# Key tiles of later batches: half tiles sent together with the queries, or quarter tiles sent one by one between them

## The chip, the cores and the metric

The kernel runs on one core of a Trainium2 chip. The metric is the device time of one execution in microseconds (us). A profiled execution was also taken; its trace gives the rows below. TensorE is called PE, VectorE DVE, ScalarE ACT, GpSimd POOL, SyncE SP. ACT and SP also issue DMAs; where a row says ACTq or SPq it is that issuing, not work of the engine.

## The reference

Four batches. In each, 12288 queries of 128 channels attend to 768 keys, which are 4x4 means of a 384x32 map times a weight; keys and values are the same. Of each batch's output rows the 128 with the highest gate score go through a small MLP and are replaced.

```python
kv_pool = kv.reshape(B, H // r, r, W // r, r, C).mean(axis=(2, 4))   # r = 4
k = v = kv_pool.reshape(B, -1, C) @ w_sr
a = softmax(q @ k.transpose(0, 2, 1) / sqrt(C)); x = a @ v
scores = einsum('bsd,d->bs', x, w_gate)                              # per batch: top 128 rows
out[top] = x[top] + sigmoid(scores[top]) * (relu(x[top] @ w1) @ w2)
```

## The kernel before

A batch is 48 blocks of 256 queries, so there are 192 blocks, numbered i = 0 to 191 through all batches. In block i PE makes the scores of block i+1 (tile `s`) and multiplies the weights of block i-4 with the values (`AV`, tile `o_two`). In between, DVE takes the row maxima (`m`), ACT the exponentials (`am`) and their high 16-bit half, and POOL the low half (both in `hl`). PE needs them transposed (`at`): 10 of the 12 128x128 tiles of each half go through a transposing DMA from SP (`turn`, two per block: the high half, then the low one), in the last batch all 12. A block's `at` must have landed when its AV begins, four blocks after its scores were used. There are five `at` buffers. SP also sends the finished rows (`out`, 256 KB, in every odd block).

Work of the next batch runs beside the blocks of the present one. Its keys come in KT = 6 tiles of 1 MB (`kv_raw`, three buffers). POOL adds the 16 taps of each key (`kv_sum`, six steps, one per block, of which the first three read `kv_raw`), so a tile takes six blocks: in batch 0 tile kc of batch 1 is read at the ends of blocks 6kc, 6kc+1 and 6kc+2; in later batches this starts five blocks into the batch. PE projects the sum (`key_tile`), and after the last tile POOL splits the values (`vx`).

Queries come 256 KB at a time (`load_q`), issued by ACT at the start of every even block, six blocks ahead. Tiles 0 to 2 of batch 1 are loaded by SP at the beginning. The other 15 tiles (`load_kv` with parts=-2) come as two halves of 512 KB, issued by ACT: the first where the generator `next_keys` reaches the tile before (two tiles before in batch 1), the second where h is 3, two blocks later; for tile 0 of batches 2 and 3 both lie in the first blocks of the batch before. Each half has a semaphore of its own (`own_load`), and POOL waits for it just before its first and second read (`landed`). The order on each engine is the order in which the code is written (`InOrder`); nothing reorders it.

Of the kernel before, what the change touches and what calls it, by code (L numbers as in the profile page):

```python
# [6 lines left out]
F32 = mybir.dt.float32  # L7
# [12 lines left out]
P = 128  # L20
B, N, C = 4, 12288, 128
HK, WK, R = 384, 32, 4
M = (HK // R) * (WK // R)
KT = M // P
TAPS = R * R
# [5 lines left out]
NBLK = N // BLK  # L31
# [40 lines left out]
def attention_topk_mlp(ctx, tc, a, outs, capacity):  # L72
    nc = tc.nc
    pe, dve, act, pool, sp = (InOrder(tc, e) for e in (nc.tensor, nc.vector, nc.scalar, nc.gpsimd, nc.sync))
# [3 lines left out]
    kvp = ctx.enter_context(tc.tile_pool(name="kvp", bufs=3))  # L78
# [49 lines left out]
    loads = {}  # L128

    def own_load(lane, out, in_):  # L130
        if lane not in lanes:
            lanes[lane] = [tc.alloc_semaphore(f"{lane[0]}{lane[1]}"), 0]
        sem = lanes[lane]
        r = act.dma_start(out=out, in_=in_)
        r.then_inc(sem[0], 16)
        sem[1] += 16
        tc.no_tile_sem_insts.add(r.ins.name)
        tc.add_to_no_dep_group(r.ins.name, r.ins)
        return sem[0], sem[1], r.ins.name

    def landed(engine, load):
        sem, count, group = load
        r = engine.wait_ge(sem, count)
        tc.declare_fence(r.ins, group=group)
        return r.ins

    def load_kv(b, kc, parts=1, t=None):
        late = t is not None
        if not late:
            t = kvp.tile([P, 2, P // 2, TAPS], F32, name="kv_raw")  # L150
        n = 2 // abs(parts)
        for i in range(abs(parts)):
            out, in_ = t[:, i * n:(i + 1) * n], a["kv"][:, b, kc, i * n:(i + 1) * n]
            if parts > 0:
                sp.dma_start(out=out, in_=in_)
            elif late == (i > 0):
                loads[b, kc, i] = own_load(("kv", (KT * b + kc) % 3 * 2 + i), out, in_)
        return t

    qraw = {}  # L160

    def load_q(b, ch, lo=0, hi=CHUNK):
        if (b, ch) not in qraw:
            qraw[b, ch] = qp.tile([P, CHUNK], F32, name="q_raw")
        out, in_ = qraw[b, ch][:, lo:hi], a["q"][:, b, ch, lo:hi]
        if (b, ch) == (0, 0):
            sp.dma_start(out=out, in_=in_)
        else:
            assert hi - lo == 2 * BLK
            blk = ch * BPC + lo // BLK  # L170
            loads[b, blk] = own_load(("q", blk // 2 % 3), out, in_)
# [201 lines left out]

    def next_keys(b):
        new_keys(b)
        raws = {}
        ready = None

        def after(kc):
            if kc % 2:  # L380
                pair = kc // 2
                start(vals, values(b, pair))
                start(splits, round_k(b, 2 * pair))

        lead, wait = (2, 0) if b == 1 else (1, 5)
        raws[0] = load_kv(b, 0, 1 if b == 1 else -2)
        if b == 1:
            raws[1] = load_kv(b, 1)
        for k in range(wait):
            yield "d"  # L390
            if k == 2:
                load_kv(b, 0, -2, raws[0])
        for kc in range(KT):
            nxt = kc + lead if kc + lead < KT and (kc or b > 1) else 0
            if nxt:
                raws[nxt] = load_kv(b, nxt, -2)
            t = raws[kc]
            pooled = kvs.tile([P, P], F32, name="pooled")
            u = kvs.tile([P, P, TAPS // 2], F32, name="kv_sum")
            t = t.rearrange("p h k t -> p (h k) t")  # L400
            by8 = [(u[:, lo:hi], t[:, lo:hi, 0:8], t[:, lo:hi, 8:16]) for lo, hi in ((0, 43), (43, 86), (86, P))]
            by4 = [(u[:, lo:hi, 0:4], u[:, lo:hi, 0:4], u[:, lo:hi, 4:8]) for lo, hi in ((0, 86), (86, P))]
            by2 = [(u[:, lo:hi, 0:2], u[:, lo:hi, 0:2], u[:, lo:hi, 2:4]) for lo, hi in ((0, 64), (64, P))]
            adds = [[x] for x in by8] + [[by4[0]], [by4[1], by2[0]], [by2[1], (pooled, u[:, :, 0], u[:, :, 1])]]
            for h, part in enumerate(adds):
                if ready and h == 2:
                    yield from key_tile(b, kc - 1, ready)
                    after(kc - 1)
                yield "d"
                if h < 2 and (b, kc, h) in loads:  # L410
                    landed(pool, loads[b, kc, h])
                for o, x, y in part:
                    pool.tensor_tensor(out=o, in0=x, in1=y, op=ALU.add)
                if kc == 0 and h == 0 and b == 1:
                    raws[2] = ahead.pop()
                if h == 3 and nxt:
                    load_kv(b, nxt, -2, raws[nxt])
            ready = pooled
        for _ in range(2):
            yield "d"  # L420
        yield from key_tile(b, KT - 1, ready)
        after(KT - 1)
# [375 lines left out]

    first_keys()

    select, prep, vals, splits, ended, ahead = [], [], [], [], [], []

    def start(tasks, gen):
        tasks.append([gen, next(gen)])
# [15 lines left out]
    n = nb - 1  # L820
# [43 lines left out]
    for i in range(nb):  # L864
        old = i >= LAG
        b, blk = blocks[i]
        if blk % 2 == 0 and i + AHEAD < nb and i + AHEAD >= BPC:
            nb_, nblk = blocks[i + AHEAD]
            load_q(nb_, nblk // BPC, nblk % BPC * BLK, (nblk % BPC + 2) * BLK)
        if blk == 0 and b + 1 < B:  # L870
            start(prep, next_keys(b + 1))
        if i == 0:
            sp.dma_start(out=w1, in_=a["w1"])
            sp.dma_start(out=w2, in_=a["w2"].rearrange("(t f) d -> f t d", f=P))
            ahead.append(load_kv(1, 2))
        if i:
            borrow(s_flat[(i - 1) % 2])
        s_max(i)
        if old:
            for j in range(QT):  # L880
                AV(i - LAG, j, halves=(0,))
            at_point("pe")
            for j in range(QT):
                AV(i - LAG, j, halves=(1,))
        else:
            at_point("pe")
        if i == 0:
            split_q(*blocks[2])
        InOrder.seen.clear()
        at_point("ev")  # L890
        bank1 = list(InOrder.seen)
        InOrder.seen.clear()
        at_point("up")
        at_point("g")
        more = 0 < i < nb - 1
        bank0 = list(InOrder.seen)
        if more:
            if not old:
                warm(12, s_flat[(i + 1) % 2][:, 1024:1024 + P], bank0 + bank1)
            free = {3: bank0 + bank1, 2: bank0, 1: bank0, 0: ()}  # L900
            for part, term in ((3, LOW), (2, LOW), (3, HIGH), (2, HIGH)):
                S(i + 1, part, term, free[part])
        exp(i, 2 if by_pe(i) else 1)
        if i < nb - 1 and by_pe(i):
            turn_pe(i)
        exp(i, 1 if by_pe(i) else 2)
        if i == nb - 1:
            st[i]["apart"] = turn_last(i, 1024, 2 * M)
            exp(i, 0)
            turn_last(i, M, 1024)  # L910
            turn_last(i, 0, M)
        InOrder.seen.clear()
        at_point("a")
        for x in InOrder.seen:
            for y in st[i + 1]["far"]:
                tc.declare_no_dep(x, y, reason="other banks")
        if more:
            for part, term in ((1, HIGH), (0, HIGH), (1, LOW), (0, LOW)):
                S(i + 1, part, term, free[part])
        to_high(i, 1)  # L920
        if old:
            sums(i - LAG)
            recip(i - LAG)
            at_point("t")
            at_point("k")
            finish(i - LAG)
        else:
            at_point("t")
        at_point("cmp")
        at_point("v")  # L930
        if i == n and quick:
            ranking = floor()
            next(ranking)
        to_low(i, 1, dve)
        if i < nb - 1:
            exp(i, 0)
        to_high(i, 0)
        if i < nb - 1:
            turn(i, 0)
            to_low(i, 0, pool)  # L940
            turn(i, 1)
        else:
            to_low(i, 0, dve)
        if i % 2 and i + 3 < nb:
            split_q(*blocks[i + 3], both=False)
        elif i % 2 == 0:
            advance(splits)
        if i and i + 3 < nb:
            low_q(*blocks[i + 3])
        at_point("d")  # L950
        if old and blocks[i - LAG][1] == NBLK - 1:
            start(select, topk(blocks[i - LAG][0]))
    ended.append(True)
    room["select"], room["count"] = banks[1], banks[0][:, 0:1]
    b = blocks[n][0]
# [237 lines left out]
```

## Time and profile before

| | us |
|---|---|
| median of three executions | 923.22 (922.45 to 926.89) |
| profiled execution | 917.34 |
| its span, first to last instruction | 915.5 |
| PE busy | 862.9 (94%) |
| DVE / ACT / POOL busy | 783.4 / 743.6 / 762.6 |

The profiled execution is the one that all rows describe: it lasted 1.84 us more than its span. PE works nearly without a break, so an idle stretch of PE in the middle is time of the kernel, whereas an idle stretch of another engine need not be.

### The profile page before, as it was taken

The numbers are of one execution on the slowest core, as the hardware profiler recorded it, in microseconds if no ns is written. First come the engines' busy times: TensorE is split into PE (matmuls) and PEld (weight loads), VectorE is DVE, ScalarE is ACT, GpSimd is POOL, SyncE is SP. The second block draws the span as 40 slices with busy tenths as digits, with TensorE's granted clock in tenths as the row PEclk, the third lists the DMA queues.
The fourth block names the chain that finished last, engine by engine and source line by source line (L and its number), as shares of the span: only waits on it lengthen the run. The fifth ranks groups of instructions, "written<-read, shape, count | busy, mean of one in ns | idle before, by whom it ended". The sixth has DMA issues, their size and how long they took to land.

```text
span 915.5 us, 21496 instructions
## 1 busy us (share of the span) xinstructions
PE 862.9 (94%) x7679; PEld 685.6 (75%) x7799; DVE 783.4 (86%) x1936; ACT 743.6 (81%) x1148; POOL 762.6 (83%) x597
## 2 busy tenths in 40 slices
PE   3898899999999999999999999999999998999996
PEld 3576777777777777777777877777777776777776
DVE  6786788888889898999878999999988998999973
ACT  2787778888888888888887888888888998989951
POOL 2698979988979999999878999999889787777752
PEclk9999999999999999999999999999999999999999
DMA  8999999999999999999999999999999999999990
GB/s 316 302 204 214 211 227 235 231 206 205 237 237 242 237 264 221 253 250 221 207 212 222 239 261 234 235 260 231 223 192 229 235 227 243 251 255 242 235 209 28
DMA packets 560479, 210.22 MB, mean 230 GB/s; under 512 B 528720, under 2 KB 530000, under 8 KB 559728
## 3 DMA queue, kind: packets, MB, share of 16 engines
q1 hardware_dynamic: 542480, 168.29, 93.6%
q10 hardware_dynamic: 17568, 39.85, 16.9%
q8 instruction: 62, 1.02, 0.5%
q0 software_dynamic: 320, 0.66, 0.3%
q14 instruction: 49, 0.40, 0.2%
HBM read 52.04 MB, written 25.49 MB: 85 GB/s over the span
## 4 chain that ended last, share of the span: by engine, by line
PE 64%; DVE 9%; DMA 9%; ACT 7%; POOL 5%; issue 4%; SPq 0%; ACTq 0%; DVEq 0%; POOLq 0%; another core or an unknown queue 0%
PE s L57 33%; PE o_two L57 31%; DMA at<-hl 7%; DVE m L57 4%; ACT am L57 4%; POOL hl L57 3%; DMA kv_raw<-in_kv 2%; ACT hl L57 2%; ACT s L57 1%; DVE o_two L57 1%; POOL ql L57 1%; DVE hl L57 1%; POOL kv_sum L57 1%; DVE junk L57 1%; DMA xe<-out,idx 1%
## 5 line engine op out<-in xcount | busy, mean ns | idle before, releaser
L57 POOL TENSOR_TENSOR hl<-am,hl 128x1280 bf16<-128x1280 f32 x191 | 501.7, 2627 | 103.4 <-ACT hl L57 49.8
L57 PE MATMUL o_two<-vx,at 128*128 128x259 f16 (+1 forms) x4548 | 424.3, 246 | 17.7 <-DMA at<-hl 11.2
L57 PEld LDWEIGHTS <-at 128*128 128x128 f16 (+1 forms) x4656 | 364.0, 97 | 98.4 <-DMA at<-hl 15.5
L57 ACT ACTIVATE am<-s,m 128x512 f32<-128x512 f32 (+1 forms) x530 | 358.9, 705 | 41.7 <-DVE m L57 26.4
L57 DVE TENSOR_REDUCE m<-s 128x2 f32<-128x1536 f32 x192 | 336.9, 1755 | 13.3 <-PE s L57 11.0
L57 ACT CAST hl<-am 128x1280 f16<-128x1280 f32 x191 | 240.6, 1260 | 6.1
L57 PE MATMUL s<-kb,ql 128*128 128x512 bf16 (+1 forms) x735 | 229.0, 324 | 4.7 <-issue 0.2
L57 PE MATMUL s<-kh,qh 128*128 128x512 f32 (+1 forms) x769 | 216.3, 377 | 1.4 <-ACT kh L57 0.7
L57 PE MATMUL s<-kl,qh 128*128 128x256 bf16 (+1 forms) x683 | 211.9, 322 | 1.2
L57 POOL TENSOR_TENSOR ql<-q_raw,qh 128x256 bf16<-128x256 f32 (+1 forms) x190 | 140.2, 738 | 2.0 <-ACT qh L57 2.0
L57 DVE TENSOR_REDUCE o_two<-o_two 128x258 f32<-128x516 f32 x188 | 128.4, 683 | 0.0
L57 PEld LDWEIGHTS s<-kh,qh 128*128 128x128 f32 x769 | 116.8, 191 | 7.0 <-ACT kh L57 0.9
L57 PEld LDWEIGHTS <-qh 128*128 128x128 bf16 x769 | 75.0, 98 | 55.3 <-issue 30.1
L57 ACT CAST at<-s 128x256 f16<-128x256 f32 x147 | 55.6, 378 | 72.5 <-PE s L57 70.4
L57 PEld LDWEIGHTS <-ql 128*128 128x128 bf16 x769 | 75.6, 98 | 25.7 <-issue 0.3
L57 DVE TENSOR_SCALAR rz<-o_two,sg 128x2 f32<-128x2 f32 x189 | 41.5, 219 | 61.8 <-PE o_two L57 59.7
L57 DVE TENSOR_TENSOR x<-o_two,rz 128x256 f32<-128x256 f32 x189 | 78.4, 415 | 0.0
L57 DVE TENSOR_TENSOR at<-s,at 128x256 bf16<-128x256 f32 x147 | 63.1, 429 | 10.3 <-ACT at L57 5.5
L57 PE MATMUL s<-cst,am 128*128 128x128 f32 x302 | 57.6, 274 | 2.4 <-ACT am L57 2.2
L57 ACT CAST qh<-q_raw 128x512 fp32r<-128x512 f32 x96 | 59.0, 615 | 0.0
L57 POOL TENSOR_TENSOR kv_sum<-kv_raw 128x344 f32<-128x344 f32 (+1 forms) x54 | 49.1, 910 | 0.0
L57 PEld LDWEIGHTS s<-cst,am 128*128 128x128 f32 x302 | 37.8, 140 | 12.2 <-ACT am L57 5.3
(162 smaller groups left out, 522.2 us busy)
## 6 DMA issues: line engine op xcount, KB each, us to landing
out<-x SPq DMA_DIRECT2D x96, 256.0 KB, 4.2
q_raw<-in_q ACTq DMA_DIRECT2D x92, 256.0 KB, 3.8
kv_raw<-in_kv ACTq DMA_DIRECT2D x30, 512.0 KB, 5.1
at<-hl SPq DMA_TRANSPOSE x382, 4.6
kv_raw<-in_kv SPq DMA_DIRECT2D x5, 1024.0 KB, 8.5
kv_raw<-in_kv SPq DMA_DIRECT2D x7, 512.0 KB, 5.4
w<-in_w SPq DMA_DIRECT2D x2, 512.0 KB, 11.4
q_raw<-in_q SPq DMA_DIRECT2D x2, 256.0 KB, 5.8
```

Source lines behind the costliest of these rows:

```text
L57: r = f(*args, **kwargs)
```

## The change

The 15 tiles that ACT loads now come as four quarters of 256 KB, each with its own semaphore (12 for keys in place of 6). They no longer hang on where `next_keys` stands: a table, `stream`, gives one quarter to every odd block: for batch 1 blocks 5, 7, ... 27 (tiles 3 to 5), for batches 2 and 3 blocks 33, 35, ... 127. ACT issues it at the start of the block. POOL waits for quarters 0 and 1 before its first read of a tile, for quarter 2 before the second and for quarter 3 before the third. Bytes, tiles, buffers and the adds themselves are as before.

```diff
         tc.declare_fence(r.ins, group=group)
         return r.ins
 
-    def load_kv(b, kc, parts=1, t=None):
-        late = t is not None
-        if not late:
-            t = kvp.tile([P, 2, P // 2, TAPS], F32, name="kv_raw")
-        n = 2 // abs(parts)
-        for i in range(abs(parts)):
-            out, in_ = t[:, i * n:(i + 1) * n], a["kv"][:, b, kc, i * n:(i + 1) * n]
-            if parts > 0:
-                sp.dma_start(out=out, in_=in_)
-            elif late == (i > 0):
-                loads[b, kc, i] = own_load(("kv", (KT * b + kc) % 3 * 2 + i), out, in_)
-        return t
+    raws = {}
+
+    def load_kv(b, kc):
+        raws[b, kc] = kvp.tile([P, 2, P // 2, TAPS], F32, name="kv_raw")
+        sp.dma_start(out=raws[b, kc], in_=a["kv"][:, b, kc])
+
+    stream = {}
+    for b in range(1, B):
+        for kc in range(3 if b == 1 else 0, KT):
+            for part in range(4):
+                stream[NBLK * (b - 1) + 8 * kc - (19 if b == 1 else 15) + 2 * part] = b, kc, part
+
+    def load_part(b, kc, part):
+        if part == 0:
+            raws[b, kc] = kvp.tile([P, 2, P // 2, TAPS], F32, name="kv_raw")
+        h, k = part // 2, part % 2 * (P // 4)
+        loads[b, kc, part] = own_load(("kv", (KT * b + kc) % 3 * 4 + part), raws[b, kc][:, h, k:k + P // 4], a["kv"][:, b, kc, h, k:k + P // 4])
 
     qraw = {}
 
@@ -373,7 +378,6 @@
 
     def next_keys(b):
         new_keys(b)
-        raws = {}
         ready = None
 
         def after(kc):
@@ -382,19 +386,13 @@
                 start(vals, values(b, pair))
                 start(splits, round_k(b, 2 * pair))
 
-        lead, wait = (2, 0) if b == 1 else (1, 5)
-        raws[0] = load_kv(b, 0, 1 if b == 1 else -2)
         if b == 1:
-            raws[1] = load_kv(b, 1)
-        for k in range(wait):
+            load_kv(b, 0)
+            load_kv(b, 1)
+        for k in range(0 if b == 1 else 5):
             yield "d"
-            if k == 2:
-                load_kv(b, 0, -2, raws[0])
         for kc in range(KT):
-            nxt = kc + lead if kc + lead < KT and (kc or b > 1) else 0
-            if nxt:
-                raws[nxt] = load_kv(b, nxt, -2)
-            t = raws[kc]
+            t = raws[b, kc]
             pooled = kvs.tile([P, P], F32, name="pooled")
             u = kvs.tile([P, P, TAPS // 2], F32, name="kv_sum")
             t = t.rearrange("p h k t -> p (h k) t")
@@ -407,14 +405,10 @@
                     yield from key_tile(b, kc - 1, ready)
                     after(kc - 1)
                 yield "d"
-                if h < 2 and (b, kc, h) in loads:
-                    landed(pool, loads[b, kc, h])
+                for x in ((0, 1), (2,), (3,))[h] if h < 3 and (b, kc, 0) in loads else ():
+                    landed(pool, loads[b, kc, x])
                 for o, x, y in part:
                     pool.tensor_tensor(out=o, in0=x, in1=y, op=ALU.add)
-                if kc == 0 and h == 0 and b == 1:
-                    raws[2] = ahead.pop()
-                if h == 3 and nxt:
-                    load_kv(b, nxt, -2, raws[nxt])
             ready = pooled
         for _ in range(2):
             yield "d"
@@ -798,7 +792,7 @@
 
     first_keys()
 
-    select, prep, vals, splits, ended, ahead = [], [], [], [], [], []
+    select, prep, vals, splits, ended = [], [], [], [], []
 
     def start(tasks, gen):
         tasks.append([gen, next(gen)])
@@ -867,12 +861,14 @@
         if blk % 2 == 0 and i + AHEAD < nb and i + AHEAD >= BPC:
             nb_, nblk = blocks[i + AHEAD]
             load_q(nb_, nblk // BPC, nblk % BPC * BLK, (nblk % BPC + 2) * BLK)
+        if i in stream:
+            load_part(*stream[i])
         if blk == 0 and b + 1 < B:
             start(prep, next_keys(b + 1))
         if i == 0:
             sp.dma_start(out=w1, in_=a["w1"])
             sp.dma_start(out=w2, in_=a["w2"].rearrange("(t f) d -> f t d", f=P))
-            ahead.append(load_kv(1, 2))
+            load_kv(1, 2)
         if i:
             borrow(s_flat[(i - 1) % 2])
         s_max(i)
```

On ACT, in blocks 4 to 6 of batch 0 (`am` is the exponential, `hl` the high half, `qh` a query split), the order before has these rows:

```order
L57 CAST hl<-am 128x1280 [waits DMAHW6_49,DMAHW5_49,Activation_49]
L57 ACTIVATE am<-s_110,m 128x512 [waits DVE_49,Pool_49]
L57 ACTIVATE am<-s_110,m 128x256
L57 CAST at<-s_110 128x256 [waits PE_49]
L57 ACTIVATE am<-s_110,m 128x768
L57 CAST hl<-am 128x1280 [waits DMAHW7_49,DMAHW0_49,Activation_49]
L57 CAST qh<-q_raw 128x512 [waits q1,Activation_sequencer_49]
L57 DMA kv_raw<-in_kv 128x1024 [waits DMAHW2_49,Pool_49]
L57 DMA q_raw<-in_q 128x512
```

and the changed kernel these:

```order
L57 CAST hl<-am 128x1280 [waits DMAHW6_49,DMAHW5_49,Activation_49]
L57 DMA kv_raw<-in_kv 128x512 [waits DMAHW2_49,DMAHW0_49,Pool_49]
L57 ACTIVATE am<-s_110,m 128x512 [waits DVE_49]
L57 ACTIVATE am<-s_110,m 128x256
L57 CAST at<-s_110 128x256 [waits PE_49]
L57 ACTIVATE am<-s_110,m 128x768
L57 CAST hl<-am 128x1280 [waits DMAHW7_49,DMAHW0_49,Activation_49]
L57 CAST qh<-q_raw 128x512 [waits q1,Activation_sequencer_49]
L57 DMA q_raw<-in_q 128x512
```

The key load of 1024 elements per partition that stood right before the query load is gone from there; one of 512 elements stands a block earlier, behind the cast of the even block and before the first exponential of the odd one. ACT has 30 rows more in all.

On POOL, at tile 3 of batch 1 (`kv0`, `kv1`, ... are the key loads' own semaphores), the order before has these rows:

```order
L57 TENSOR_TENSOR kv_sum<-kv_raw 128x344 [waits kv0,Pool_sequencer_49]
L57 TENSOR_TENSOR hl<-am,hl 128x1280 [waits DMAHW2_49,DMAHW1_49,Activation_49]
L57 TENSOR_TENSOR ql<-q_raw,qh 128x256 [waits Activation_sequencer_49,PE_49,Activation_49]
L57 TENSOR_TENSOR kv_sum<-kv_raw 128x344 [waits kv1,Pool_sequencer_49]
L57 TENSOR_TENSOR hl<-am,hl 128x1280 [waits DMAHW4_49,DMAHW3_49,Activation_49]
L57 TENSOR_TENSOR ql<-q_raw,qh 128x256
L57 TENSOR_TENSOR kv_sum<-kv_raw 128x336
```

and the changed kernel these:

```order
L57 TENSOR_TENSOR kv_sum<-kv_raw 128x344 [waits kv0,kv1,Pool_sequencer_49]
L57 TENSOR_TENSOR hl<-am,hl 128x1280 [waits DMAHW2_49,DMAHW1_49,Activation_49]
L57 TENSOR_TENSOR ql<-q_raw,qh 128x256 [waits Activation_sequencer_49,PE_49,Activation_49]
L57 TENSOR_TENSOR kv_sum<-kv_raw 128x344 [waits kv2,Pool_sequencer_49]
L57 TENSOR_TENSOR hl<-am,hl 128x1280 [waits DMAHW4_49,DMAHW3_49,Activation_49]
L57 TENSOR_TENSOR ql<-q_raw,qh 128x256
L57 TENSOR_TENSOR kv_sum<-kv_raw 128x336 [waits kv3,Pool_sequencer_49]
```

No instruction of POOL moves; the waits are four per tile where they were two. The rows of PE, DVE and SP stand in the same order as before.

## Rows read from the trace of the kernel before

**Rows 1.** The page's part 1: engine, busy us, share of the span, instructions.

```profile
PE 862.9 (94%) x7679; PEld 685.6 (75%) x7799; DVE 783.4 (86%) x1936; ACT 743.6 (81%) x1148; POOL 762.6 (83%) x597
```

**Rows 2.** What PE waited for, 45 to 880 us: total us, times, longest.

```profile
PE o_two L57 <- DMA at<-hl: 11.2, 12, 2.6
PE o_two L57 <- POOL vx L57: 3.0, 2, 1.9
```

**Rows 3.** The same for 60 to 120, 280 to 400, and 700 to 880 us.

```profile
PE o_two L57 <- DMA at<-hl: 7.0, 5, 2.6
...
PE o_two L57 <- DMA at<-hl: 1.9, 5, 0.8
...
PE o_two L57 <- DMA at<-hl: 2.2, 2, 1.4
```

**Rows 4.** Timeline of PE at its two longest waits: start, us, operation, [idle before <-releaser].

```profile
87.70 0.85 PE L57 MATMUL o_two<-vx,at 128*128 128x130 f16 x12 [2.63 <-DMA at<-hl]
...
110.68 3.83 PE L57 MATMUL o_two<-vx,at 128*128 128x259 f16 x24 [2.60 <-DMA at<-hl]
```

**Rows 5.** Three stretches: busy us by engine, PE clock, DMA share, GB/s.

```profile
60.30:121.40 61.10, 53.80 (x458) 42.02 (x464) 44.97 (x87) 45.07 (x69) 50.86 (x42) 0.97 1.17 216
130.40:182.50 52.10, 51.68 (x459) 41.41 (x465) 45.04 (x88) 45.05 (x69) 50.48 (x42) 1.00 1.16 232
110.70:114.10 3.40, 3.40 (x20) 2.62 (x21) 0.00 (x0) 0.56 (x2) 3.35 (x3) 0.50 1.20 344
```

**Rows 6.** Row maxima (one per block) in the first two stretches: count, ns, starts.

```profile
L57 DVE TENSOR_REDUCE m<-s x12: 1757/1758/1759, 60.3 to 116.8; 128x2 f32<-128x1536 f32 x12
...
L57 DVE TENSOR_REDUCE m<-s x12: 1758/1758/1759, 130.4 to 178.2; 128x2 f32<-128x1536 f32 x12
```

**Rows 7.** Transposes, 60 to 120 us: issue ns min/median/max, then landing us.

```profile
L57 SPq DMA_TRANSPOSE at<-hl x24: 1282/1834/5197, 56.6 to 119.4; - x24
...
DMA to landing us min/median/max: 3.1/5.5/10.9
```

**Rows 8.** The same, 150 to 240 us, a stretch without key loads.

```profile
L57 SPq DMA_TRANSPOSE at<-hl x43: 1252/1636/3497, 149.1 to 239.9; - x43
...
DMA to landing us min/median/max: 3.1/4.4/6.8
```

**Rows 9.** The same, 280 to 400 us, with nine key loads.

```profile
L57 SPq DMA_TRANSPOSE at<-hl x53: 1271/1647/4193, 279.7 to 398.6; - x53
...
DMA to landing us min/median/max: 3.2/4.9/9.2
```

**Rows 10.** Loads issued by ACT, timeline around 78 us.

```profile
78.08 0.33 ACTq L57 DMA_DIRECT2D kv_raw<-in_kv  x1
78.44 1.32 ACTq L57 DMA_DIRECT2D q_raw<-in_q  x1
```

**Rows 11.** Key loads by ACT, whole kernel; 60 to 120; 280 to 400 us: count, issue ns, starts.

```profile
L57 ACTq DMA_DIRECT2D kv_raw<-in_kv x30: 334/334/825, 52.1 to 609.1; - x30
...
L57 ACTq DMA_DIRECT2D kv_raw<-in_kv x4: 334/334/352, 69.5 to 108.6; - x4
...
L57 ACTq DMA_DIRECT2D kv_raw<-in_kv x9: 334/334/370, 282.3 to 391.0; - x9
```

**Rows 12.** The page's part 6: DMA issues, KB each, median us to landing.

```profile
q_raw<-in_q ACTq DMA_DIRECT2D x92, 256.0 KB, 3.8
kv_raw<-in_kv ACTq DMA_DIRECT2D x30, 512.0 KB, 5.1
```

**Rows 13.** Timeline of ACT at the start of an odd block.

```profile
56.19 1.26 ACT L57 CAST hl<-am 128x1280 f16<-128x1280 f32 x1
57.85 1.05 ACT L57 ACTIVATE am<-s,m 128x512 f32<-128x512 f32 x2 [0.41 <-DVE m L57]
```

**Rows 14.** Timeline of POOL around the first read of a key tile.

```profile
120.89 0.73 POOL L57 TENSOR_TENSOR ql<-q_raw,qh 128x256 bf16<-128x256 f32 x1
121.58 0.91 POOL L57 TENSOR_TENSOR kv_sum<-kv_raw 128x344 f32<-128x344 f32 x1
```

## The prediction

> **What bounds the kernel now.** I read the page's table of engines first, then PE's waits, then the timeline at those waits, and last the DMA issues around them. PE is busy for 862.9 of 915.5 us [rows 1], so between 45 and 880 us only what stops PE counts. What stops it there most is the transposed weights: 11.2 us in 12 waits [rows 2]. They are bunched: 7.0 us in five waits between 60 and 120 us, 1.9 us in five between 280 and 400 us, and 2.2 us in two after 700 us [rows 3]. The longest two are 2.63 and 2.60 us [rows 4]. The second has a sequel: right after it the granted clock is 0.50, so 1.2 instead of 2.4 GHz, for 3.4 us in which PE works without a break [rows 5].
>
> The same loss shows in the length of the blocks. Twelve row maxima, so twelve blocks, start between 60.30 and 121.40 us and twelve between 130.40 and 182.50 us [rows 6]; the first dozen takes 61.10 us, the second 52.10 us [rows 5]. Both have key sums on POOL (50.86 and 50.48 us busy); what only the first has is key loads on the move. In the second PE is busy 51.68 of 52.10 us: that is the pace without waits, 52.10/12 = 4.34 us per block.
>
> Why the transposes are late then: without key loads the longest issue on SP is 3.5 us and the slowest landing 6.8 us [rows 8], and PE never waits; with four key loads in 60 us it is 5.2 and 10.9 us [rows 7], with nine in 120 us 4.2 and 9.2 us [rows 9]. SP's queue is in order, so one stretched issue holds back the transposes behind it. A key load never comes alone: the 512 KB issued at 78.08 us have the 256 KB of queries right behind them, and that second issue itself takes 1.32 us [rows 10] against 0.33. So 768 KB start in one spot while the SP queue needs the same engines.
>
> **The change part by part.** *The early waits.* In batch 0 four halves are issued from 69.5 to 108.6 us [rows 11]: 2 MB in 39 us, or nine blocks at 4.34 us. Now 256 KB come in every second block, 1 MB in eight blocks, and never beside a query load. That is about half the density and a third of the largest burst. In the stretch 280 to 400 us nine halves, 4.5 MB, came in 120 us, which is 28 blocks at 4.34 us, so 1.3 MB in eight blocks [rows 11], and the waits were 1.9 us in all. The new density is below that, so I expect nearly all 7.0 us gone, and with the 2.60 us wait its half clock: 3.4 us at half speed hold 1.7 us of full-speed work, so 1.7 us come back. Together 8.7 us; the pace gives 61.10 - 52.10 = 9.0 us for the same thing. I take 8.5 us. Bounds: 9.0 us if nothing is left, and 2.60 + 1.7 = 4.3 us if only the later of the two long waits goes (a rival, below).
>
> *The later waits.* 1.9 us between 280 and 400 us. I count 1.0 us: the density falls only from 1.3 to 1.0 MB per eight blocks, and part of what PE gains before a batch's end it loses at the next batch's first AV, where it waited for POOL's split of the values (two waits, 3.0 us [rows 2]); POOL, with 50.48 of 52.10 us busy [rows 5], can hardly run ahead. Bounds 0 and 1.9 us. The 2.2 us after 700 us stay: no key load is left there (the last issue is at 609.1 us [rows 11]).
>
> *Loads where there were none.* Blocks 33 to 47 and 80 to 95 had none and get a quarter in every odd block. Without key loads the landings have room: 6.8 us at worst, no waits [rows 8]. I take 0. The upper end is the rate of the loaded stretch, 1.9 us per 120 us [rows 3], over these 31 blocks or 135 us: 2.1 us. The lower end is 0, as there is no wait to lose.
>
> *ACT.* 30 issues more (60 for 30) of 334 ns [rows 11] are 10.0 us of its sequencer. They stand behind the cast of 1.26 us of the even block; the next exponential begins 0.41 us after that cast's end because it waits for DVE [rows 13]. So 0.33 us lie under 1.67 us and cost nothing. If that cover were gone, all exponentials of the odd block and with them PE's next scores would be 0.33 us late, 60 times, but 30 of the old ones go from the even blocks: 0 to 10.0 us, and I take 0. A quarter also waits on ACT until POOL has read the tile three before it. By the table that read lies at least two blocks earlier (the tile for blocks 57 to 63 was read until block 55), 8.7 us, so it has happened. Behind that wait would stand the exponentials and thus PE.
>
> *POOL.* 60 waits for 30. A wait passes in the sequencer while the 0.73 us operation before it runs, and the sum starts with no idle [rows 14]; I take 0. The far end is an added wait that takes all of those 0.73 us, 30 times, 22 us. The data is there: the shortest lead is that of batch 1's tile 5, whose last quarter is issued at block 27 and read at the end of block 32, over five blocks or 21.7 us against a landing of 5.1 us for twice the size [rows 12]. PE, DVE and SP lose and gain no instruction.
>
> The Trainium skill, page "DMA: Bandwidth & Descriptors", section "Rules for kernel authors", speaks against small pieces: 128 partitions and at least 1 MiB per DMA. The rows agree that pieces cost: 256 KB land in 3.8 us and 512 KB in 5.1 us [rows 12], so two quarters need 7.6 us for one half, 2.5 us more, 75 us over 30 halves. By the page's fit of about 2.0 us fixed per DMA it would be an estimated 60 us. By either, all of it is latency that lies within leads of five blocks and more, and I count none of it.
>
> **The sum.** 917.34 us for the profiled execution (span 915.5 and 1.84 around it) - 8.5 - 1.0 + 0 + 0 + 0 = 907.8 us. The median before, 923.22 us, is 5.9 us longer than that execution. I carry this over: 913.7 us, 1.0% less.
>
> **The rivals.** *Half of it stays.* SP may be behind already when the first quarter starts, from the loads at the kernel's start. Then the waits before 90 us stay, the 2.63 us one among them [rows 4], and of those 7.0 us only the 2.60 us go. For it: by 87.70 us only three halves had been sent, at 52.1, 69.5 and 78.1 us [rows 10, 11]. Against: that wait comes right after the half of 78.08 us, and the second dozen of blocks shows that SP can catch up. Gain 2.60 + 1.7 + 1.0 = 5.3 us, 917.9 us.
>
> *No change.* What slows the transposes is the bytes beside them, not their bursts: the mean DMA share is 1.16 to 1.17 in the stretch with and in the one without key loads [rows 5], so there is no idle room that spreading could use. The same 3 MB then cost the same 8.7 us as more and shorter waits, and the later ones their 1.9: 923.2 us. Against: the 12 waits are the five, five and two of the three stretches [rows 2, 3], so before 700 us none lies where no key load is on the move. The same page's section "Queues, rings and completion order" says that each DMA engine takes turns between queue rows packet by packet; by that rule a transpose shares with every load packet, whenever it comes, which is this rival.
>
> *Slower.* The quarter starts in the odd block, where SP also sends the 256 KB of finished rows. If quarter, rows and two transposes don't fit into 4.34 us, the second transpose of each odd block lands late, and from blocks 33 to 127 there is no quiet stretch left to catch up. Price: 48 odd blocks at the mean later wait, 1.9/5 = 0.38 us, is 18.2 us, less 8.5: 9.7 us more, 932.9 us. It decides once landings over 6.8 us recur in odd blocks. For it: 9.2 us occurs at a density only a third higher [rows 9]. Against: that stretch lost only 1.9 us.
>
> *The change does not do what it says*, so that a quarter waits on ACT for its buffer: the leads above leave at least two blocks, and I give it no chance of its own.
>
> **How the numbers follow.** Forecast 0.62, half stays 0.17, no change 0.14, slower 0.07. About 0.5%, 4.6 us, is what a measurement of this kernel tells from no change. The forecast lies below 918.6 us but for a tail; of the rival at 917.9 us about 0.6 lies below. Faster 0.62 - 0.01 + 0.10 = 0.71; same 0.01 + 0.07 + 0.14 = 0.22; slower 0.07. Range 908.5 to 920.5 us: below, all early and later waits gone (9.0 + 1.9 = 10.9 us, 912.3 us) and 3.8 us more in case the 5.9 us by which the plain runs exceed the profiled one are partly the same waits; above, the rival at 917.9 us and the 2.1 us of the newly loaded stretches, with a margin. It leaves out the slower case, most of no change and a small tail below.
>
> **What would show it.** In the profile after: no wait of PE for `at` over 0.5 us between 60 and 120 us; no half clock near 110 us; twelve blocks from about 60 us in under 54 us; longest landing of a transpose there under 8 us; 60 key loads of 256 KB; ACT's and POOL's idle time as before. It would be wrong if waits of PE for `at` appear between 140 and 250 us, or if their sum to 700 us stays over 5 us.

## The result, and the profile after

Over 20 executions of each kernel the changed kernel takes 907.85 us (median; 901.36 to 914.06) and the kernel before 919.24 us (907.84 to 926.89). The measured ratio, here and in every experiment below, is one of fast executions alone and so not the quotient of the medians (0.9876 here): it is 0.9909, 95% interval 0.9888 to 0.9930. That is 0.9% faster, 1.0% was forecast. The three executions known before (median 923.22 us) were on the long side; 0.9909 of them is 914.8 us against the 913.7 us forecast, while the plain median of 907.85 us lies 0.65 us below the stated range.

The profiled execution took 909.29 us, its span 907.5 us. PE's waits from 45 to 880 us (total us, times, longest) answer [rows 2]:

```profile
PE o_two L57 <- DMA at<-hl: 5.5, 7, 1.7
PE o_two L57 <- POOL vx L57: 3.0, 2, 1.9
PE o_two L57 <- DVE x L57: 2.7, 6, 0.8
PE s L57 <- DMA xe<-out,idx: 2.4, 2, 1.2
PE s L57 <- ACT am L57: 0.9, 1, 0.9
PE s L57 <- DMA at<-hl: 0.6, 1, 0.6
```

The same from 695 to 880 us has 5.5 us in all seven waits: every wait of `o_two` for `at` is now in the last batch, which has no key loads, and none is left before it. The blocks that answer to [rows 5, 6] (row maxima, then the two stretches of twelve blocks with PE, PEld, DVE, ACT, POOL, the PE clock, DMA share, GB/s):

```profile
L57 DVE TENSOR_REDUCE m<-s x12: 1756/1758/1758, 58.9 to 106.7; 128x2 f32<-128x1536 f32 x12
```

```profile
58.90:110.90 52.00, 51.58 (x458) 41.35 (x464) 44.94 (x87) 44.93 (x69) 50.09 (x41) 1.00 1.20 238
119.90:172.00 52.10, 51.68 (x459) 41.41 (x466) 45.01 (x88) 45.04 (x69) 50.49 (x42) 1.00 1.17 236
```

The first dozen now runs at the pace of the second: 52.00 us in place of 61.10, with the clock at 1.00 in place of 0.97. The DMA share there rose from 1.17 to 1.20 and the rate from 216 to 238 GB/s: not quite the same bytes (13.2 and 12.4 MB) move in less time. The transposes, issue in ns and landing in us, at 60 to 120, 150 to 240 and 280 to 400 us, answer to [rows 7 to 9]:

```profile
L57 SPq DMA_TRANSPOSE at<-hl x27: 1279/1673/3513, 59.3 to 117.3; - x27
...
DMA to landing us min/median/max: 3.6/5.0/7.1
...
L57 SPq DMA_TRANSPOSE at<-hl x43: 1309/1862/3332, 147.5 to 239.9; - x43
...
DMA to landing us min/median/max: 3.2/5.1/8.9
...
L57 SPq DMA_TRANSPOSE at<-hl x57: 1269/1615/4572, 279.2 to 399.2; - x57
...
DMA to landing us min/median/max: 3.6/4.7/7.5
```

The longest landings of these loaded stretches fell (10.9 to 7.1, 9.2 to 7.5 us); that of the once quiet stretch rose (6.8 to 8.9 us), and PE does not wait there either. From 45 to 695 us the longest is 9.3 us, in batch 2. What the key loads themselves look like (issues in ns, landing), and one of them on ACT's timeline:

```profile
L57 ACTq DMA_DIRECT2D kv_raw<-in_kv x60: 334/334/392, 46.3 to 586.6; - x60
...
DMA to landing us min/median/max: 3.0/4.1/7.4
```

```profile
63.76 1.26 ACT L57 CAST hl<-am 128x1280 f16<-128x1280 f32 x1
63.77 0.34 ACTq L57 DMA_DIRECT2D kv_raw<-in_kv  x1
65.43 1.05 ACT L57 ACTIVATE am<-s,m 128x512 f32<-128x512 f32 x2 [0.41 <-DVE m L57]
```

The issue lies under the cast, and the exponential waits the same 0.41 us for DVE as in [rows 13].

By blocks (start of the row maximum of the first to that of the last; each difference is of these starts):

| blocks | before, us | after, us |
|---|---|---|
| 4 to 28 | 113.0 | 104.4 |
| 28 to 48 | 87.0 | 87.0 |
| 48 to 96 | 215.3 | 212.6 |
| 96 to 144 | 217.3 | 217.9 |
| 144 to 188 (last batch) | 189.6 | 193.4 |

So this pair of executions gained 8.6 us in batch 0 and 2.7 us in batch 1, and lost 3.8 us in the last batch, where the work is the same. Another 1.9 us lie before block 4 (it starts at 43.4 and at 41.5 us), ahead of the first load that was changed, and are no gain of the change. From block 4 to block 144, where the key loads are, the execution after is 10.8 us shorter (632.7 and 621.9 us). Of these, 8.9 us are the waits for `at` that are gone and an estimated 1.7 us the half clock.

### The profile page after: what moved, and what is told of

The parts are those of the page before. It is cut to its first block, busy times and chain, and to the rows that moved or that the text cites. A ratio compares the mean times of both kernels' runs of the same rounds, so it can differ in the third digit from the quotient of the medians.

```text
span 907.5 us, 21555 instructions
## 1 busy us (share of the span) xinstructions
PE 860.2 (95%) x7679; PEld 684.9 (75%) x7799; DVE 783.6 (86%) x1936; ACT 743.5 (82%) x1148; POOL 762.5 (84%) x597
## 4 chain that ended last, share of the span: by engine, by line
PE 70%; DVE 9%; DMA 7%; ACT 6%; POOL 4%; issue 3%; SPq 0%; ACTq 0%; DVEq 0%; POOLq 0%; another core or an unknown queue 0%
PE s L57 37%; PE o_two L57 34%; DMA at<-hl 4%; DVE m L57 4%; ACT am L57 3%; POOL hl L57 2%; DMA kv_raw<-in_kv 2%; ACT hl L57 1%; DMA xe<-out,idx 1%; ACT s L57 1%; DVE hl L57 1%; DVE o_two L57 1%; DVE junk L57 1%; POOL ql L57 1%; DVE x L57 0%
## 5 line engine op out<-in xcount | busy, mean ns | idle before, releaser
L57 DVE TENSOR_REDUCE m<-s 128x2 f32<-128x1536 f32 x192 | 336.8, 1754 | 13.2 <-PE s L57 10.9
## 6 DMA issues: line engine op xcount, KB each, us to landing
w<-in_w SPq DMA_DIRECT2D x2, 512.0 KB, 12.4
```

Of the source, the lines that this page charges most:

```text
L57: r = f(*args, **kwargs)
```

## The experiments

Twelve runs, one of them the changed kernel again, were each timed in five rounds against the kernel before. The first question was which property of the change gives the time: smaller pieces, lower density, or loads that no longer start together. The fences give each edit in short; the slices, the semaphores and POOL's waits follow it.

**Halves in odd blocks.** The changed kernel with tiles in two pieces:

```diff
-            for part in range(4):
-                stream[... + 2 * part] = b, kc, part
+            for part in range(2):
+                stream[... + 4 * part] = b, kc, part
```

> The same table with halves of 512 KB, one in every fourth block, in odd blocks, so never beside a query load: the density of the changed kernel (1 MB in eight blocks), twice its burst. Theory burst (the waits came from how much starts in one spot, 768 KB before, 256 KB now): between the two, 0.993 to 0.997 of before, with some us of PE's waits for at back between 60 and 250 us. Theory density (2 MB in nine blocks before, 1 MB in eight now, whatever the pieces): as the changed kernel, 0.991, no wait over 0.5 us at 60 to 120 us.

Measured 0.9978 (0.9940 to 1.0016). Slightly above the burst theory's range, clearly not the density theory's 0.991, which the interval leaves out. PE's wait for `at` from 45 to 695 us:

```profile
PE o_two L57 <- DMA at<-hl: 2.7, 5, 1.4
```

These waits are not all that this execution lost. PE's longest wait is one for `xe`, the rows gathered for the MLP, and the clock is at half for 6.8 us from shortly before its end:

```profile
448.96 0.45 PE L57 MATMUL s<-cst,xe 128*128 128x128 f32 x1 [3.74 <-DMA xe<-out,idx]
...
448.10:454.90 6.80, 5.94 (x28) 4.21 (x29) 2.10 (x8) 2.99 (x6) 0.67 (x1) 0.50 1.12 247
```

PE works for 5.94 us of that stretch, which at half speed is an estimated 3.0 us lost. What held the gather up is not shown.

**Halves in even blocks, spaced.**

```diff
-    (19 if b == 1 else 15) + 2 * part,  range(4),  load after load_q
+    (18 if b == 1 else 14) + 4 * part,  range(2),  load before load_q
```

> Halves of 512 KB in even blocks with the query load right behind, as before, but one in every fourth block: the burst of before (768 KB) at the density of the changed kernel. Theory burst: 0.997 to 1.0 of before, waits of PE for at of 4 us or more between 60 and 120 us. Theory density: 0.991, as the changed kernel.

Measured 1.0107 (1.0069 to 1.0144): slower than before, which neither theory had forecast. Even spacing of this burst is no gain. The same wait:

```profile
PE o_two L57 <- DMA at<-hl: 5.4, 10, 1.4
```

Only 0.4 us of them lie before 220 us, where 4 us or more were expected between 60 and 120 us. The profiled execution is also the fastest of the twelve (919.95 us; their median is 926.85), so it shows less than the typical loss.

How the kernel before loads explains this in part; the prediction had read it wrongly. A key load stands beside a query load there only in batch 0 (six halves, all right ahead of one, as in [rows 10]) and at the first half of tile 0 of batches 2 and 3. The other 22 of the 30 halves start in odd blocks, more than 4 us from the queries on either side:

```profile
260.87 0.34 ACTq L57 DMA_DIRECT2D q_raw<-in_q  x1
...
265.03 0.33 ACTq L57 DMA_DIRECT2D kv_raw<-in_kv  x1
...
269.41 0.34 ACTq L57 DMA_DIRECT2D q_raw<-in_q  x1
```

So this kernel does not only space the old burst of 768 KB: it brings that burst to batches 1 and 2, which had 512 KB at a time. That fits waits which hardly come in batch 0 and come later. That it costs the whole 1.07% isn't shown.

**Quarters in the old place.** The kernel before, with each half cut in two:

```diff
-loads[b, kc, i] = own_load(("kv", (KT * b + kc) % 3 * 2 + i), out, in_)
+for x in range(2):
+    k = slice(x * P // 4, (x + 1) * P // 4)
+    loads[b, kc, 2 * i + x] = own_load(..., t[:, i, k], a["kv"][:, b, kc, i, k])
```

> The kernel before with each half of 512 KB as two quarters of 256 KB issued one right after the other at the old place: piece and semaphores of the changed kernel, burst and density of before. Both theories: 0.998 to 1.002 of before. Rival piece size (smaller DMAs let the transposes through better): 0.991 to 0.995.

Measured 1.0017 (0.9974 to 1.0060), as both theories said. The piece size by itself is worth nothing that could be measured; the waits are those of the kernel before (8.9 us in the same stretch):

```profile
PE o_two L57 <- DMA at<-hl: 10.1, 12, 2.1
```

**No key loads on ACT.**

```diff
-            t = raws[b, kc]
+            t = raws[1, kc % 3] if (b, kc) not in raws else raws[b, kc]   # and an empty table
```

> Leaves out the 15 key loads issued by ACT: the tiles of batch 1 loaded at the start are summed again in their place. The ceiling of what the loads cost. Theories burst and density: 0.987 to 0.991, since the changed kernel's profile has no wait of PE for at left between 45 and 700 us. Rival bytes (what the loads move costs time wherever it stands): 0.985 or less, because the changed kernel would still pay for 15 MB.

Measured 0.9879 (0.9840 to 0.9917). No wait of PE for `at` in this stretch, and the transposes land in at most 6.8 us:

```profile
L57 SPq DMA_TRANSPOSE at<-hl x293: 1252/1501/3616, 44.4 to 692.4; - x147
...
DMA to landing us min/median/max: 2.9/4.4/6.8
```

So 1.2% is about all that the 15 MB cost, and the change takes back 0.9 of these 1.2 points (the two intervals overlap). The rival by which the bytes cost time wherever they stand wanted 0.985 or less, which the interval still touches; the quarters beside the queries, below, decide against it.

**Where the time comes from.** The table for batch 1 alone, then for batches 2 and 3 alone (the others load halves as before):

```diff
-    for b in range(1, B):
+    for b in (1,):        # second kernel: (2, 3)
```

> Quarters by the table for batch 1 alone (blocks 5 to 27); batches 2 and 3 load halves as before. By the prediction's terms 8.5 of 9.5 us come here: 0.990 to 0.992 of before, no wait of PE for at between 60 and 120 us. Rival: the plain runs lose as much in the later batches as in the first, then 0.994 to 0.997.

> Quarters by the table for batches 2 and 3 alone (blocks 33 to 127); batch 1 loads halves as before. By the prediction's terms 1.0 us: 0.998 to 1.0 of before, the waits at 60 to 120 us stay. Rival, as above: 0.994 to 0.997.

Measured 0.9954 (0.9920 to 0.9989) and 0.9958 (0.9915 to 1.0002). By the values, both times the rival: the parts gain about alike, and together (0.9912) what the whole change gains. The first interval leaves out the 0.9907 that 8.5 us would give; the second holds the rival's range and the prediction's 0.998 to 1.0. Of the 24 halves that the second kernel replaces, 22 stood apart from the queries before (shown above); what it changes for them is the size, 256 KB at a time in place of 512, and the even spacing. In the first kernel's profile the waits that are left lie between 283 and 311 us, in the second's between 91 and 112 us; the rows, in this order:

```profile
PE o_two L57 <- DMA at<-hl: 1.4, 3, 0.9
```

```profile
PE o_two L57 <- DMA at<-hl: 2.7, 4, 1.7
```

**Quarters beside the queries.**

```diff
-    (19 if b == 1 else 15) + 2 * part,  load after load_q
+    (18 if b == 1 else 14) + 2 * part,  load before load_q
```

> The changed kernel with every quarter one block later, in the even blocks, right before the query load: 256 + 256 KB in one spot, nothing in the odd blocks. Burst by ACT's loads alone: as halves in odd blocks (512 KB in one spot), 0.996 to 1.0 of before. Rival (what matters is the size of one DMA or being apart from the finished rows that SP sends in odd blocks): 0.99 or less, as the changed kernel or better.

Measured 1.0000 (0.9960 to 1.0040): one block later, right ahead of the queries, and the whole gain is gone. Same pieces, same density. The wait, its longest instance with the clock after it, and the queries' issues and landings:

```profile
PE o_two L57 <- DMA at<-hl: 7.5, 7, 2.5
```

```profile
397.38 0.86 PE L57 MATMUL o_two<-vx,at 128*128 128x130 f16 x12 [2.54 <-DMA at<-hl]
```

```profile
397.40:401.70 4.30, 4.30 (x25) 3.04 (x26) 2.25 (x9) 1.24 (x3) 2.34 (x5) 0.60 1.28 188
```

```profile
L57 ACTq DMA_DIRECT2D q_raw<-in_q x72: 334/474/1792, 51.5 to 694.4; - x72
...
DMA to landing us min/median/max: 3.1/4.9/9.4
```

**Eighths in every block.**

```diff
-            for part in range(4): ... + 2 * part
+            for part in range(8): ... + part
```

> Eighths of 128 KB, one in every block, each with its own semaphore, so beside the query load in even blocks: 128 KB in odd and 384 KB in even blocks against 256 and 256 KB; 60 issues more on ACT. Burst theory: the largest burst grows from 256 to 384 KB, 0.993 to 0.996 of before. Rival (the smaller the pieces the better): 0.988 to 0.991.

Measured 0.9912 (0.9875 to 0.9949), no wait for `at` before 700 us. 128 KB behind a query load cost nothing that could be measured; the expectation of the burst theory was wrong here, and smaller pieces were no better either.

**Once more, and two cuts of the queries.**

> The changed kernel once more, beside the next three on the same chip: 0.989 to 0.993 of before. In its profile no wait of PE for at between 45 and 700 us (with the waits after 700 us at 2 to 6 us, as in the other profiles).

Measured 0.9891 (0.9846 to 0.9935); 0.2 us of waits before 700 us, 6.1 us after.

```diff
-        if blk % 2 == 0 and ...: load_q(..., blk of 2 * BLK columns)
+        every block: load_q(..., BLK columns), own semaphore each
```

> The changed kernel with the query loads also cut: 128 KB in every block in place of 256 KB in every even one; keys stay 256 KB in odd blocks. So 384 KB start together in odd blocks, 128 KB in even ones. Burst theory: no loss up to 384 KB, so 0.989 to 0.992 before 700 us; in the last batch, where queries are the only loads of ACT, the largest start falls from 256 to 128 KB and the waits there (2.5 to 6.6 us so far) fall below 2 us: 0.986 to 0.990 in all. Rival (the waits of the last batch come from the 12-tile transposes themselves): 0.990 to 0.993, waits there as before.

Measured 0.9875 (0.9834 to 0.9917). The value lies in the range expected for 128 KB, but not for the reason given: in the last batch (695 to 880 us) the waits did not fall below 2 us:

```profile
PE o_two L57 <- DMA at<-hl: 4.1, 6, 1.5
```

The same with the keys in eighths:

> Queries 128 KB and keys 128 KB in every block: 256 KB start in each block, the evenest of all. Burst theory: 0.986 to 0.990, as query halves or a little better. Rival (90 issues more on ACT and smaller rows cost something, or the last batch is as before): 0.991 to 0.995.

Measured 0.9871 (0.9837 to 0.9905), 3.8 us of waits in the last batch. On the same chip the changed kernel has 0.9891 with an interval that holds both; neither can be said to beat it.

**Quarters in four consecutive blocks.**

```diff
-                stream[... + 2 * part] = b, kc, part
+                stream[... + part] = b, kc, part
```

> The changed kernel with the four quarters of a tile in four consecutive blocks and then four without: 1 MB in four blocks, two of the four quarters right behind a query load. Burst theory (largest start 512 KB, in half of the quarters): 0.996 to 1.0. Density theory (twice the local density of the changed kernel): 0.998 or more. Neither: 0.991.

Measured 0.9881 (0.9843 to 0.9919): as good as the change, where both theories had put it near 1.0. The wait, and the queries' issues and landings beside those of the quarters in even blocks above:

```profile
PE o_two L57 <- DMA at<-hl: 0.9, 1, 0.9
```

```profile
L57 ACTq DMA_DIRECT2D q_raw<-in_q x72: 334/335/382, 52.7 to 685.8; - x72
...
DMA to landing us min/median/max: 3.1/3.7/5.5
```

**What they show together.** Beside each other: what ACT starts in one spot where a key load is, PE's wait for `at` in the profile from 45 to 695 us, the time from block 4 to block 144 in the same execution (starts of the row maxima), and the measured ratio:

| kernel | in one spot, KB | wait, us | blocks 4 to 144, us | ratio |
|---|---|---|---|---|
| before | 768 in batch 0, then 512 | 8.9 | 632.7 | 1 |
| halves, even blocks, before the query | 768 | 5.4 | 631.1 | 1.0107 |
| quarters, old place | 768 in batch 0, then 512 | 10.1 | 633.6 | 1.0017 |
| quarters, even blocks, before the query | 512 | 7.5 | 632.3 | 1.0000 |
| halves, odd blocks | 512 | 2.7 | 629.9 | 0.9978 |
| late only | 768 in batch 0, then 256 | 2.7 | 623.2 | 0.9958 |
| early only | 256 in batch 0, then 512 | 1.4 | 622.1 | 0.9954 |
| eighths, every block | 128 and 384 | 0 | 621.4 | 0.9912 |
| changed kernel (two runs) | 256 | 0 / 0.2 | 621.9 / 622.4 | 0.9909 / 0.9891 |
| quarters, four blocks running | 256 and 512 | 0.9 | 621.7 | 0.9881 |
| query halves / all eighths | 384 / 256 | 0 / 0 | 623.5 / 622.5 | 0.9875 / 0.9871 |
| no key loads | - | 0 | 620.2 | 0.9879 |

(The two first halves of tile 0, which stand beside a query, are left out of "then 512".) The ratio is of many executions, the two columns before it of one: the profile of `halves, even` was the fastest of twelve, that of `no key loads` the fastest of six.

The kernels with hardly a wait have the gain, those with several us have not. That the waits for `at` are what the change removes is shown, and that neither smaller pieces alone nor even spacing alone does it. `Halves, odd` and `late only` have the same 2.7 us and lie 6.7 us apart: the wait for `xe` (3.7 us) and the half clock (3.0 us) shown above are about as much, so the waits for `at` are not the whole of what an execution loses. Where 512 KB or more start in every spot the gain is missing, and where 384 KB or less do it is there; `quarters, four blocks running`, with 512 KB in every second spot, does not fit that. Not settled, then, is why a key piece in an even block costs nothing in two kernels and everything in two others. They differ in two things at once: in `quarters, even` and `halves, even` the key load stands ahead of the query load (as before the change in batch 0) and comes in every second or fourth block without a pause; in the four blocks running and in the eighths it stands behind the query load, and the former pauses for four blocks after each tile. With the key load ahead (quarters, even blocks) the query's issue is stretched to as much as 1.79 us and the query lands in 4.9 us at the median; with it behind (four blocks running), at most 0.38 and 3.7 us. Quarters in even blocks behind the query load would tell order from amount; this was not run.

## Why the prediction was right

*The waits go, and with them the half clock.* Right in the profile: 7.0 us of waits at 60 to 120 us became none, twelve blocks fell from 61.10 to 52.00 us (9.1 us; 8.5 were counted and 9.0 given as the bound), and no half clock is left there. PE's busy time in all fell from 862.9 to 860.2 us. Not all of these 2.7 us are the change's: besides the half clock at 110.70 us the execution before has a second one at the kernel's start, where nothing was changed, and the execution after has none there:

```profile
25.40:28.80 3.40, 3.18 (x13) 2.02 (x13) 2.22 (x4) 1.05 (x2) 0.52 (x2) 0.50 0.99 390
```

The landings at 60 to 120 us stayed under 8 us, as was said.

*Why the transposes were late: true of batch 0 alone.* "A key load never comes alone" holds for the six halves of batch 0 and two more, and with it "a third of the largest burst" and the title's "sent together with the queries". The other 22 halves stood apart from the queries already, as the rows of the halves in even blocks show, so that for them the change is smaller pieces, evenly spaced. The prediction put the 1.9 us of 280 to 400 us down to density alone and did not see that they came at 512 KB in one spot.

*The early and the later waits, 8.5 and 1.0 us: both mis-sized.* Alone, the later batches' table gives 0.42%, or 3.9 us of 919.24, and the early one 0.46%, or 4.2 us (intervals of 0 to 7.8 and of 1.0 to 7.4 us). One term was about twice too large and the other about four times too small, by these values. That the two add up to a forecast so near the measured ratio is in part luck. The split of 8.5 to 1.0 read one execution as if it were typical. The kernel with quarters in the old place shows how little that holds: with the same bursts and much the same total, blocks 4 to 28 have 2.6 us of waits and blocks 48 to 144 have 7.5 us, where the kernel before had 7.0 and 1.9. In `late only`, whose batch 0 loads as before, blocks 4 to 28 take 107.3 us, 2.9 us more than after the change, where the kernel before took 8.6 us more. The bursts are fixed; where a transposed tile comes too late differs from execution to execution. The loss that was expected at a next batch's first AV did not grow: 3.0 us before and after. Waits of up to 2.6 us that stand in one profile were worth summing, not worth placing.

*Newly loaded stretches, 0.* Right: blocks 28 to 48 take 87.0 us as before, though landings now reach 8.9 us. The point given for the slower rival, landings over 6.8 us, was passed here and at 280 to 400 us without a cost, so that threshold was wrong; the rival itself did not come.

*ACT and POOL, 0.* Right: 60 issues of 334 ns lie under the casts, as the timeline above shows, and twelve blocks with POOL's key sums and its added waits run at the pace of [rows 5].

*The last batch, unchanged.* Not so in this pair: 2.2 us of waits before, 5.5 after. In the other profiles they are between 2.6 and 6.6 us, 3.1 without any key loads and 5.6 and 5.7 with half of the change, so the two executions differ there by no more than such profiles do; that the change has no part in it isn't shown.

*The 5.9 us carried over.* Wrong: with 20 executions the median before is 919.24 us, 1.9 us over its profile, and the median after is 1.4 us under its own. The 5.9 us came from three executions that were on the long side. That is why the plain median after lies just under the range, while the ratio came out as forecast.

*The rivals.* "Half stays" and "no change" did not come. The mechanism named for "no change", that bytes cost alike wherever they stand, is refuted by moving quarters one block: same bytes, 1.0000 against 0.9909. The Trainium skill's turns of the queue rows packet by packet ("DMA: Bandwidth & Descriptors", "Queues, rings and completion order") are therefore not enough to forecast a wait: the two kernels share the DMA engines by the same rule. Its advice against pieces below 1 MiB ("Rules for kernel authors") is right in latency (two quarters at 4.1 us each, above, against 5.1 us [rows 12], so 3.1 us more per half where the prediction had 2.5) and beside the point here, since POOL waits for no key load between 45 and 695 us: eighths of 128 KB cost no time. The fit behind the prediction's 60 us stands on the same page of the Trainium skill ("Anatomy of one DMA") for DMAs that GpSimd issues; these are issued by ACT, so it was a rough guide at most.

## What to carry to other kernels

Where a queue of small transfers is needed just in time and big loads are not, cut the loads and start them apart from each other; cutting alone, or spacing alone, gave no clear gain here. The place of the pieces beside other loads decided in one pair of kernels between all of the gain and none of it, at the same bytes; in others a piece beside a query load cost nothing, and why is open. A profile's sum of waits can be used to size a gain, but test with an experiment where in the program it arises. And list what stands beside each load in the whole trace before calling one pair of rows the rule: here the rule held for 8 of 30.

## What the runs showed of the hardware

A long wait of PE is not always followed by the lower clock. After 2.60 us (before, at 110.68 us) and 2.54 us (quarters in even blocks, at 397.38 us) the granted clock went to 1.2 GHz for 3.4 us (0.60 on average over 4.3 us is 3.4 us at 0.50); after waits of 2.63 us in the kernel before [rows 4] and in the halves in even blocks it stayed at 2.4 GHz. The rows of these last two, first the wait and the clock in the halves in even blocks, then the clock in the kernel before:

```profile
792.95 0.86 PE L57 MATMUL o_two<-vx,at 128*128 128x130 f16 x12 [2.63 <-DMA at<-hl]
```

```profile
793.00:797.00 4.00, 4.00 (x36) 3.08 (x37) 3.09 (x10) 2.95 (x4) 2.52 (x3) 1.00 1.21 221
```

```profile
87.70:91.10 3.40, 3.35 (x30) 2.63 (x32) 2.17 (x7) 1.25 (x3) 1.74 (x3) 1.00 1.21 268
```

Nor does the length of the wait sort the others: with 3.74 us (halves in odd blocks, above) the clock went to 1.2 GHz for 6.8 us, after 1.99 us (halves in even blocks, at 450.31 us, for `xe`) for 3.4 us, and after 2.23 us (quarters in even blocks, at 815.02 us) it stayed.

And two loads issued one behind the other on ACT hold each other up in the issue: the second of them took up to 1.79 us instead of 0.33, whichever it was (the query behind a key quarter, above, or up to 1.09 us the key quarter behind a query in the four consecutive blocks):

```profile
L57 ACTq DMA_DIRECT2D kv_raw<-in_kv x60: 334/374/1091, 48.4 to 576.7; - x60
```
